# A new order table behind the first transfers in a fused attention and two-MLP kernel

## The chip, the cores and the metric

The kernel runs on one core of a Trainium2 chip. The metric is the device time of one execution in microseconds (us). Five engines work side by side, each through its own queue and in the order of that queue: PE (TensorE, the matmuls), DVE (VectorE), ACT (ScalarE), POOL (GpSimd) and SP (SyncE, which here only issues transfers).

## The reference

Attention over 4 batches, 8 heads, 576 positions and 64 channels, with a causal window; its output is the input of two MLPs, one behind the other, of 2304 rows.

```python
def _attn_ref(q, k, v):
    scores = scale * np.matmul(q, k.transpose(0, 1, 3, 2))
    rel = pos[:, None] - pos[None, :]
    mask_plain = (rel >= 0) & (rel < window)                 # window = 32, heads 0 to 3
    mask_dil = (rel >= 0) & (rel < window * dilation) & (rel % dilation == 0)   # dilation = 4, heads 4 to 7
    ...
    return np.matmul(attn, v)          # softmax of the masked scores, times v

def reference(...):
    x = attn_out.transpose(0, 2, 1, 3).reshape(2304, 512)
    x = np.maximum(x @ moe_w_in, 0.0) ** 2 @ moe_w_out       # 512 -> 2048 -> 512
    h = x @ moe2_w_in                                        # 512 -> 2048
    return (h * (1.0 / (1.0 + np.exp(-h)))) @ moe2_w_out     # -> 512
```

## The kernel before

**Arithmetic.** PE computes with pairs: a fp32 value is held as a hi part (the rounded cast, `copy`, L245 on ACT, L247 on DVE, L249 on POOL) and a lo part (the residual, `sub`, L252, on DVE or POOL). A product is three matmuls: hi·hi, hi·lo, lo·hi. So everything that PE multiplies has to pass through a cast and then a residual on the other engines.

**Weights.** Each piece (one of 16 chunks of 128 hidden columns, input half or output half) arrives as 64-bit numbers and is made into fp32 by integer steps in `weights()`: scale the upper word (L282 on ACT, L284 on DVE or POOL), scale the lower word (L290 on ACT, L292 elsewhere), shift (L302 on DVE or L304 on POOL), set the sign (L311 or L314, DVE), add (L318), then cast and residual. ACT, DVE and POOL can do several of these; the order table picks.

**Attention.** It runs in 8 half-batches of 4 pairs of heads. A block is: scores (L533, PE), mask and row maximum (L558, DVE), exp (L566, ACT), scale (L590 on ACT), transposes, p·v on PE. The first 8 blocks are the "early" ones of `late_exp()`: there the row maximum is subtracted, transposes come first (L713 or L715 and L717) and exp follows them (L729, ACT); p·v is L738 on PE, its row sums are treated at L744 and L746 (DVE), and the normalised result is `xn` (one L751 on DVE, or one L754 for each unit on ACT: three or four). PE transposes `xn` (L625, L630), and a cast and a residual make the MLP's input `x`.

**MLP 1** has tiles of 256, 256, 256, 512, 512 and 512 rows. The first three run chunk by chunk side by side: an up-projection (`s1`, L788 to L790), ReLU (L804) and square (L810) on ACT, cast (L245) and residual (L252) into `g`, a down-projection (`s2`, L836 to L838). Later tiles and MLP 2 (three tiles of 768 rows) use sums of weights that are prepared in between (L389, L417, `st`) so that fewer products are needed (L936, L990 to L992, L1094, L1179). In MLP 2 the Silu (L1130) runs on ACT.

**The order.** Nothing is scheduled at run time. `Planner.order()` (L119) reads the text table `ORDER` (L1358 to L1606): each word is an engine's letter (P, A, V for DVE, G for POOL, D for a transfer), a step's number, and places in memory behind `@`. `run()` (L1308) emits the steps in this order, so an engine's queue is the sequence of its letters. A word `F` is a filler: so many matmuls on a zero tile (L1245), whose result nobody reads. A POOL step waits for the last locked DVE step ahead of it in the table (`turn`). Two dummy activations of one column (L1302 to L1306), one Exp and one Silu, are steps of the table too; the compiler puts an `ACT_TABLE_LOAD` where the needed function changes.

```python
            if word[0] == "F":
                o = self.filler(int(n))
                o.eng = "PE"
            else:
                o = self.ops[int(n)]
                o.eng = {"P": "PE", "A": "ACT", "V": "DVE", "G": "Pool", "D": "DMA"}[word[0]]
```

Of the kernel before, what the change touches and what calls it, by code (L numbers as in the profile page):

```python
# [1359 lines left out]
P10@3 P36@28@1 V17 V50 P67@36@2 G20 A12 V38 A11 V49 V37 D65@156 V48 P13@0 V39 V68 V40 D95@152 P21@1 F3@3 V51 A22  # L1360
P41@2 A23 D96@160 V35 V14 P24@3 V71 A43 V15 G127@0 V70 A42 A16@2 V81 D398@196 V79 P52@1 V69 V82 P44@2 V80 A53
V25 A54 V72 A136@4 P55@0 V26 V45 V66 V46 A27 V83 D143@52 P98@40@3 V56 V138 A47@6 V57 P28@1 G129 P73@3 V100
A29@44 F3@2 V58 A74 V101 D160@76 P59@2 V111 A31@48 V99 P84@3 V32 A62 V30 A60 P75@0 A85 V102 V61 A128 F3@1 V63
V110 D152@56 P86@2 V76 V103 A137 V77 V112 P104@1 A78@8 V113 V87 F7@3 V97 V114 V88 A105 V130 D177@88 A89 P115@1
V139 P106@0 A116 V131 F1@2 P90@3 D169@80 P117@2 V140 A91@60 A93@64 A132@68 F5@1 V94 V92 A141@164 V107 V118
P400@3@1@72@0 V108 V119 D211@124 G133 A153@14 V109@12 V120 A162 V403 F2@2 V401 A145 P121@0 G142 V402 V410
D506@201 P404@2 V411 A122 A144@10 V123 V412 A154 V146 P1238@3 D186@92 V399 A161@2 V147 A170@0 V148 P413@1 A124
A405 V178@4 D220@128 A149@84 V125 V163 A1239@16 P406@0 V150 A414 A1240 V164 P415@2 A179 D194@108 V407 V155
P1244@3 A1241@6 V408 V165 A409@8 V416 V156 A166@100 D424@196 P507@0@1@96@1 V417 V1242 A418 V157 P1243 A1245@18
V167 A158@168 D151 V172 A1246 V510 A187@10 D134 P419@3 V159 P1250@2 A422@104 A420 V512 A1247@12 G189 V508 V423  # L1370
A513 V421 A171 D203@116 V1248 P426@3@0@112@2 V180 A1251@16 V173 A511 P1249 A509 V427 G174 V523 A1252 V428 A188
V429 V436 V438 A1253@14 P430@2 V525 A524 V437 V514 V521 A526 V515 V425 V1254 A522 P439@1 V190 A431 A516 V527
A517 V175@172 P432@3 V528 V176 A440 A529 P518@0 V530 A222 P441@2 V433 V181 A204@2 P531@1 P1255 V434 V442 A520
V182 A435@8 V443 V519 A533 V444 D539@196 A532 A183@120 V191 P534@3 A195@6 V184 P445@0 A537@12 A535 V446 P1256@1
A192@176 G197 V448 V536 A196 V447 D450@201 V449 V198 A205 V193 A1257@18 P540@0@3@20@3 A1258 V199 A1259@4 D237@40
A212@0 V1260 V554 A200@28 P1261 V556 G206 V545 A557 V558 V543 A555 D254@76 V541 V201 A559 P452@0@3@24@0 A542
V560 V207 A544 A546 V561 D538 V451 P1262@1 V208 D271@112 A562 A563 V547 V465 V548 V455 A549 V466 G550 V454
P564@2 V463 A1263@16 D228@36 V464 A565 V456 A1264 V453 A566 V209@180 P551@1 A1265@8 V214 P457@2 A552 A553 V210
A221@14 D245@72 P567@1 V215 A458 A213 V223 P467@0 V1266 A238@12 V216 P459@3 A568 A468 V224 D572@196 A570@4
A217@32 P469@2 V240 A229@10 V225 P1267 A256 V460 V470 V461 V471 G218 V462@6 A239 D478@201 V472 A246@8 V569  # L1380
P473@0 V231 P1274@1 A476@52 A474 V241 A230 V475 A226@184 D262@92 V477 V232 P573@3@0@56@1 A1275@18 V227 A1276
A1277@2 V233 D296@116 A255@6 P480@1@2@80@2 V589 V587 A234@88 G1278 V580 V593 V576 A590 V574 G235 V591 P1279 A247
V483 D305@24 V484 V482 A592 V481 V493 A575 V492 V494 A581 P485@0 V578 V491 A577 D202 V248 A588 V263@10 P495@3
A579 V242 A486 A594 V582 P1286@0 A243@188 V583 D279@108 V479 V595 V584 A272@0 V596 V249 P585@1 V597 A1287@16
P487@2 D219 V244 A586 A496 P598@1 V250 A1288 D571 P497@3 D288@124 A599 V488 A1289@2 V489 P600@0 A490@14 V498
V1290 V499 V251@96 P1291 V257 A500 V252 D605@201 A603@4 V265 P501@2 V258 P1298@1 A504 A502 V601 A280@8 D638@196
V503 V505 V274 P1268@3 V602 A1299@18 V275 A1300 D322@56 A264 V259 P606@2@1@20@3 A273 V266 A1301@12 P1280@0
A1269@16 D604 V611 G281 D313@80 V609 V626 A1270 V620 V624 A610 V607 V267 A625 P1292@3 A1271@2 V613 A260@192 V622
V1302 A290 V261 P1304@2 A1281@18 V282 A612 V1272 A621 V268@128 A1293@16 V276 P639@1@36@0 A1294 A614 V269 A623
P640@3 A627 A1282 V628 V641 P1273 A608 V645 A1283@14 V615 V652 V629 G1284 V616 V654 A630 V643 V656 P1303 V289@2  # L1390
V617 A1305@18 A297@4 V291 V292 P618@0 A1295@6 P1285 A642 V1306 A646 V293 A619 A298 V283 P631@0 P1310@2 A657
V277@132 A653 V284 A632 D339@124 V1296 A285@40 P633@0 V278 A655 V299 P1297 A644 A634 D185 V647 V286 A294@136
A1307@14 V635 D666@201 P1316@1 A1311@16 V306@6 A1312 V648 V658 A636@10 V659 V1308 A660 V295 P1322@2 D287
V1550@12 A649 D637 V308 A1317@18 V1551@2 P661@0 A1313@0 P650@3 P1309 A662 V307 A315 V1314 V1552@112 A651 V324
A1318 P667@3@76@1 V1554@108 A1323@16 V1553 A1324 V300 A1319@8 P663@1 A314@10 V669 P668@0 V1555 V673 A664@2 V1320
P1328@2 V682 V671 V680 D694@196 A672 V684 V316 A674 P1334@3@0@1 V301 A670 A1329@18 V309 A302@72 D665 V675 A1330
P1315 V676 D253 A685 V677 A1559 V303 D330@92 A1331@12 A1556 P678@2 V1332 P1321 V323@0 A1325@14 V317 A681 A679
V1326 A683 P1340@2 V1562@8 A1335@16 A1336 V310 V686 P695@3@20@2 V1563@2 A1341@18 A1342 V687 V1560 A688 P696@2
V701 V703 G1564@116 V697 A702 P1333 V712 A311@144 V714 V1557 A1337@4 D1561 A704 V699 V710 P1327 A715 V325 A700
V1338 V716 V318 D1558 P689@3 A1343@14 V312 P1346@2 A698 A711 V705 V341 A690 V706 V1565 A717 P1352@3 V707  # L1400
A1347@16 A1348 V1566@36 A713 V1344 A319@68 V1567 P708@2 P1339 V326 A709 A1353@18 V320 A1568 D347@112 V718
A1349@2 P691@2 V719 V1574@10 A1354 A1571 V720 P1345 A1355@8 V327 A340@12 A692@6 V342 D726@201 P721@3 V1572
P1358@2 A722 A328@140 V1350 V1575@14 P1364@3 V1356 A1359@16 V329 D1573 A1360 A331@4 V1576@24 V1578@84 P1370@2
A1361@0 V1577 A1365@18 V1569 D693 A1366 A1580 D356@108 V1362 P727@3@80@3 V1579 A1371@16 V343 A1583 P1351 A1372
V733 D1570 V731 V729 V735 V344 A736 P723@2 A734 V1584 A345@148 P728@3 V333 A730 V1581 A1367@10 P1357 A732 V1368
A724@6 V742 D758@196 A332 V746 V737 V748 V744 V357@14 P1382@2 A745 V738 A749 V739 D1585 A743 V334 A747 P740@3
A1383@18 V358 P1363 A741 V335 A1373@2 D364@36 A1384 V750 A336@116 V751 V359 P759@3@2@76@0 V1374 A1385@8 V337
A752 D321 P1369 V773 V762 D725 V760 A348@0 V775 V764 D1582 A761 V1386 P1376@3 V350 A763 V349 A765 V777 A774 V766
V346 D168 A778 P753@2 A1377@16 P1375 V767 V351 A768 A1378 V769 A754 V360 D270 A365@4 P770@2 P1388@3 V1586@10
A1379@6 A776 V771 A772 V361 D236 P755@2 V1380 A1389@18 V779 V1587@12 A1390 P1381 A756@2 V780 V367 D373@56  # L1410
A362@152 V782 A781 V1588@100 V352 P783@2 P1400@3 A784 V1590@20 D390@84 A353@24 V1589 A785 V1591 P1406@2 V354
A1401@16 A1391@10 D757 A1402 V1599@0 D381@92 A1403@12 V1392 P1394@3 A366 V1404 A1407@18 V363 A1595 D789@201 V368
P1387 A1408 A1395@16 V1598@6 A1396 A1409@14 V369 D338 P1418@3 V1410 A370@120 V1600@124 A1592 V1602@80 V1601
P786@2 A1419@18 V371 A1420 P1393 V1603 A1397@8 A787@0 V1398 A1604 V1593 A374@6 D820@196 P1412@3 V1596 A1607
V1605 A1421@10 V391@4 P1399 A1413@16 D1594 V1608 A1414 V393 A1415@2 V383 P790@3@2@108@1 V394 A382@8 D788 A375
D372 V384 P1405 V791 V804 G1416 A792 V806 V795 V793 V808 A794 P1424@3 D355 V376 A796 A807 D1646@112 V797 V798
V1422 P1436@2 V800 A1425@18 V377 A799 A1426 D1609 V1610@12 P801@3 A1437@16 V378 P1411 A802 A803 A809 V1611@0
D1597 A1438 A805 V1614@76 P821@3@2@100@2 A1427@14 V810 V1612@28 V811 P1423 A812 V822 G813 D1606 V824 A823 V826
V828 A825 V1428 A827 V839 P814@3 V835 G1613 V837 P1429 A816 D1655@80 A829 V1615 A815 A1616 V841 V830 V831 A842
P817@3 V832 A1439@0 P833@2 V1440 A818@12 V385 A840 P1442@3 A836 V1623@10 A838 A379@156 V843 V1617 D819 A1619  # L1420
# [253 lines left out]
```

## Time and profile before

| | |
|---|---|
| time, median of 3 runs | 849.27 us (848.89 to 849.51) |
| the profiled execution's own time | 849.5 us |
| its span in the profile | 847.7 us |
| PE busy | 839.2 us (99%) |
| DVE busy | 638.8 us (75%) |
| ACT busy | 501.5 us (59%) |
| POOL busy | 122.2 us (14%) |
| granted TensorE clock, mean | 0.999 |

A busy share is a mean over the whole span. The windows in the rows below give the same for stretches, and the timelines give single instructions: start, duration, engine, line, and in brackets how long the engine had been idle and what ended the idle time. On DVE and ACT neighbours overlap in the record by about 0.1 us, so what a step occupies is read from start to start.

### The profile page before, as it was taken

To read this page: it belongs to the slowest core of one execution; us is meant where nothing else is said; L and a number is where in the kernel's file an instruction comes from. 1 tells how busy PE (TensorE), PEld (TensorE's weight loads), DVE (VectorE), ACT (ScalarE), POOL (GpSimd) and SP (SyncE) were. 2 spreads that over 40 slices of the span, in tenths; PEclk is the share of its full clock that TensorE was granted. 3 is DMA by queue.
4 is the path that set the end of the run, shared out by engine and by line. 5 is a ranking of instruction groups with operands and counts; after the bars stand their busy time and mean duration, and the time that the engine had idled before them with its cause. 6 is when DMAs were issued, how large, how long until landed. Compare 5 with 4: busy or idle time off the path is not lost.

```text
span 847.7 us, 16967 instructions
## 1 busy us (share of the span) xinstructions
PE 839.2 (99%) x6009; PEld 795.6 (94%) x6009; DVE 638.8 (75%) x1706; ACT 501.5 (59%) x1324; POOL 122.2 (14%) x142
## 2 busy tenths in 40 slices
PE   9989999999999999999999999999999999999998
PEld 7879999999989889889998999999999999999998
DVE  6999999888888698768899997578722488422765
ACT  5999988887666265334542566565445555345652
POOL 2220000101210202131201002102201111202020
PEclk9999999999999999999999999999999999999999
DMA  9585568879898888988999989889774774773441
GB/s 344 178 284 207 152 204 304 278 265 333 310 303 318 308 292 282 326 311 288 336 344 299 343 308 351 301 287 324 248 259 149 246 266 164 269 262 111 174 159 65
DMA packets 83603, 223.56 MB, mean 264 GB/s; under 512 B 8768, under 2 KB 18240, under 8 KB 83520
## 3 DMA queue, kind: packets, MB, share of 16 engines
q1 hardware_dynamic: 83520, 222.49, 75.2%
q8 instruction: 47, 0.77, 0.3%
q14 instruction: 36, 0.29, 0.1%
HBM read 172.13 MB, written 50.33 MB: 262 GB/s over the span
## 4 chain that ended last, share of the span: by engine, by line
PE 94%; ACT 3%; DVE 1%; issue 0%; POOL 0%; POOLq 0%; ACTq 0%
PE y L1094 17%; PE sa L1179 15%; PE s L936 15%; PE y L1179 6%; PE y L990 5%; PE y L991 5%; PE y L992 5%; PE sa L1094 4%; PE s L788 3%; PE s L789 2%; PE s L790 2%; PE ax L533 2%; PE y L836 2%; PE ax L625 2%; PE y L837 2%; PE y L838 2%
## 5 line engine op out<-in xcount | busy, mean ns | idle before, releaser
L245 ACT CAST hl<-gq 128x384 fp32r<-128x384 f32 x168 | 79.5, 513 | 58.7 <-PE sa L1179 28.6
L1094 PE MATMUL y<-xs,ws 128*128 128x384 f32 x552 | 107.5, 334 | 0.0
L252 DVE TENSOR_TENSOR hl<-gq,hl 128x384 fp32r<-128x384 f32 x144 | 78.9, 581 | 27.3 <-ACT hl L245 24.0
L1094 PEld LDWEIGHTS y<-xs,ws 128*128 128x128 f32 x552 | 96.6, 188 | 0.1
L1065 DVE TENSOR_TENSOR gq<-y,gq 128x384 f32<-128x384 f32 x46 | 25.0, 554 | 94.1 <-PE y L1094 82.9
L1070 ACT COPY gq<-y 128x384 f32<-128x384 f32 x92 | 42.7, 479 | 75.0 <-PE y L1094 67.6
L1179 PE MATMUL sa<-hl,wp 128*128 128x384 f32 x432 | 79.1, 334 | 0.0
L936 PE MATMUL s<-x,ws 128*128 128x256 f32 x576 | 76.2, 284 | 0.0
L990 PE MATMUL y<-g,w 128*128 128x512 f32 x192 | 76.2, 397 | 0.0
L1179 PEld LDWEIGHTS sa<-hl,wp 128*128 128x128 f32 x432 | 75.2, 188 | 0.0
L991 PE MATMUL y<-g,w 128*128 128x512 f32 x192 | 75.2, 392 | 0.0
L992 PE MATMUL y<-g,w 128*128 128x512 f32 x192 | 74.9, 390 | 0.0
L952 DVE TENSOR_TENSOR h<-s,h 128x512 f32<-128x512 f32 x96 | 59.4, 619 | 19.8 <-PE s L936 16.6
L936 PEld LDWEIGHTS s<-x,ws 128*128 128x128 f32 x576 | 72.2, 191 | 1.2
L245 ACT CAST g<-r 128x256 fp32r<-128x256 f32 (+1 forms) x86 | 42.9, 504 | 51.2 <-DVE r L972 42.8
L566 ACT ACTIVATE ap<-ap,ast 96x128 f32<-96x128 f32 (+3 forms) x168 | 62.2, 371 | 8.3 <-DVE ast L575 4.2
L788 PE MATMUL s<-x,w 128*128 128x256 f32 x192 | 56.4, 294 | 0.1
L790 PE MATMUL s<-x,w 128*128 128x256 f32 x192 | 54.3, 283 | 0.0
L789 PE MATMUL s<-x,w 128*128 128x256 f32 x192 | 54.2, 282 | 0.0
L1179 PE MATMUL y<-hl,sw 128*128 128x384 f32 x288 | 51.4, 334 | 0.0
L1179 PE MATMUL sa<-hl,sw 128*128 128x384 f32 x288 | 50.9, 334 | 0.0
L1179 PEld LDWEIGHTS y<-hl,sw 128*128 128x128 f32 x288 | 50.0, 188 | 0.0
(176 smaller groups left out, 2071.2 us busy)
## 6 DMA issues: line engine op xcount, KB each, us to landing
raw<-w SPq DMA_DIRECT2D x64, 512.0 KB, 6.3
ws<-w1x SPq DMA_DIRECT2D x48, 512.0 KB, 6.7
ws<-w2x SPq DMA_DIRECT2D x48, 512.0 KB, 5.4
sw<-w2y SPq DMA_DIRECT2D x48, 512.0 KB, 4.5
wa<-w1s SPq DMA_DIRECT2D x24, 512.0 KB, 6.8
wa<-w2s SPq DMA_DIRECT2D x24, 512.0 KB, 5.7
w1x<-st SPq DMA_DIRECT2D x16, 512.0 KB, 4.8
w2x<-st SPq DMA_DIRECT2D x16, 512.0 KB, 5.1
```

What stands on the lines that cost most here:

```text
L245: self.nc.scalar.copy(out=out, in_=in_)
L252: self.eng[eng].tensor_tensor(out=out, in0=a, in1=b, op=ALU.subtract)
L566: es.append(self.op({"ACT": c_act(nk) + 0.185}, lambda e, i=i, n=n, c=c, p=p, st=st: nc.scalar.activation(out=p.tile[:n, c], in_=p.tile[:n ...
L788: nc.tensor.matmul(o, wh.tile[:, s], xh, start=(kk == 0), stop=False)
L789: nc.tensor.matmul(o, wh.tile[:, s], xl, start=False, stop=False)
L790: nc.tensor.matmul(o, wl.tile[:, s], xh, start=False, stop=(kk == KC - 1))
L936: nc.tensor.matmul(bank.tile[:, o:o + 256], wp, xp, start=i == 0, stop=last, skip_group_check=True)
L990: nc.tensor.matmul(o, wh.tile[:, s], gh.tile, start=c == 0, stop=False)
L991: nc.tensor.matmul(o, wh.tile[:, s], gl.tile, start=False, stop=False)
L992: nc.tensor.matmul(o, wl.tile[:, s], gh.tile, start=False, stop=(c == NF - 1))
L1094: nc.tensor.matmul(o, w[part == 2].tile[:, kk * P:kk * P + P], x[b][part == 1].tile[:, kk * half:kk * half + half], start=new and not kk a ...
L1179: nc.tensor.matmul(o, u.tile[:, c * P:c * P + P], v.tile, start=new and not q and not part, stop=q == nf - 1 and part == 2, skip_group_che ...
```

## The change

Only the table `ORDER` differs (L1360 to L1606). Its first line and the first words of the next stay, so the first 16 transfers are as before; behind them the words stand in another order. No step is added or removed: 750 PE steps and 516 transfers in both. 182 steps change engine: 81 from ACT to DVE, 55 from DVE to ACT, 36 from POOL to DVE, 10 from POOL to ACT. Steps by engine are 1092 before and 1076 after on ACT, 1479 and 1541 on DVE, 123 and 77 on POOL. The fillers have 53 matmuls before (groups of 14, 15, 3, 3, 3, 7, 1, 5, 2) and 58 after (14, 15, 3, 3, 3, 8, 6, 6), the last six ahead of the down-projection of chunk 3. Places in memory change with the order. The first differing line:

```diff
-P10@3 P36@28@1 V17 V50 P67@36@2 G20 A12 V38 A11 V49 V37 D65@156 V48 P13@0 V39 V68 V40 D95@152 P21@1 F3@3 V51 A22
...
```

Place one, DVE at about 23 to 26 us, ahead of the first up-projection. The row `x<-ax,x 128x4x64` is the last residual of `x` that this up-projection needs; `cv`, `raw` are weight pieces. Before:

```order
L558 ISA ap,ast<-ax,mask 96x128
L558 ISA ast 96x1
L558 ISA ap,ast<-ax,mask 96x128
L558 ISA ast 96x1
L252 TENSOR_TENSOR x<-ax,x 128x4x64
L558 ISA ap,ast<-ax,mask 96x128
L558 ISA ast 96x1
L302 TENSOR_SCALAR cv<-cv 128x512
L510 MEMSET blk 128x6
L311 SCALAR_TENSOR_TENSOR cv<-raw,cv 128x512
L318 ISA cv<-raw,cv 128x1024
L284 TENSOR_SCALAR cv<-raw 128x512
```

In the changed kernel there is first, a little earlier in the queue:

```order
L302 TENSOR_SCALAR cv<-cv 128x512
L252 TENSOR_TENSOR x<-ax,x 128x4x64
L744 TENSOR_SCALAR ast<-ax 72x4
L318 ISA cv<-raw,cv 128x1024
L746 RECIPROCAL ast<-ast 72x4
L510 MEMSET blk 128x6
L744 TENSOR_SCALAR ast<-ax 72x4
L751 TENSOR_TENSOR xn<-ax,ast 72x4x64
L746 RECIPROCAL ast<-ast 72x4
```

and then, around the same residual:

```order
L558 ISA ast 96x1
L558 ISA ap,ast<-ax,mask 96x128
L558 ISA ast 96x1
L311 SCALAR_TENSOR_TENSOR cv<-raw,cv 128x512
L252 TENSOR_TENSOR x<-ax,x 128x4x64
L302 TENSOR_SCALAR cv<-cv 128x512
L558 ISA ap,ast<-ax,mask 96x128
L558 ISA ast 96x1
L318 ISA cv<-raw,cv 128x1024
L311 SCALAR_TENSOR_TENSOR cv<-raw,cv 128x512
```

One `L302` and the `blk` memset stand ahead of the residual now, one `L311` right ahead of it, and the two `xn` are separate, with a row sum's reciprocal between them.

Place two, ACT from about 19 to 25 us. `x<-ax 128x4x64` (the second such row) is the cast whose residual was shown above. Before:

```order
L754 ACTIVATE xn<-ax,ast 72x64 x4
L729 ACTIVATE ap<-ax 72x288
L245 CAST x<-ax 128x4x64
L245 CAST x<-ax 128x4x8
L245 CAST w_467<-cv 128x512
L245 CAST w_478<-cv 128x512
L282 ACTIVATE cv<-raw 128x512
L290 ACTIVATE raw<-raw 128x512 x2
L245 CAST x<-ax 128x4x64
L282 ACTIVATE cv<-raw 128x512
L290 ACTIVATE raw<-raw 128x512
L282 ACTIVATE cv<-raw 128x512 x2
```

After:

```order
L282 ACTIVATE cv<-raw 128x512
L245 CAST x<-ax 128x4x8
L245 CAST x<-ax 128x4x64
L729 ACTIVATE ap<-ax 72x288
L290 ACTIVATE raw<-raw 128x512
L245 CAST w_478<-cv 128x512
L282 ACTIVATE cv<-raw 128x512 x2
L290 ACTIVATE raw<-raw 128x512
L282 ACTIVATE cv<-raw 128x512
L245 CAST x<-ax 128x4x64
L282 ACTIVATE cv<-raw 128x512
L245 CAST w_535<-cv 128x512
```

More `L282` and `L290` weight steps stand ahead of that second cast, and one weight cast (`w`) and one set of four `L754` fewer.

Place three, ACT in the middle of MLP 1, where the dummy Silu (L1304) stands. Before it was much later, ahead of the first `L1130`:

```order
L1070 COPY gq<-y_8110 128x384
L1070 COPY gq<-y_8127 128x384
L245 CAST st<-st 128x2x256 x2
L1304 ACT_TABLE_LOAD
L1304 ACTIVATE first<-warm 128x1
L1070 COPY gq<-sa 128x384
L1130 ACTIVATE gq<-gq 128x768
```

After, with attention's exp (L566) still to come:

```order
L566 ACTIVATE ap,ast<-ap,ast 96x128
L590 ACTIVATE ap<-ap,ast 96x128 x3
L245 COPY ap<-ax 128x288
L1304 ACT_TABLE_LOAD
L1304 ACTIVATE first<-warm 128x1
L245 CAST x_5571<-stg 128x512
L245 CAST x_5581<-stg 128x512
L245 CAST x_5585<-stg 128x512
L245 CAST x_5611<-xr 128x512
```

Some rows later the table for exp is loaded again:

```order
L245 CAST g_5745<-r 128x512
L245 CAST st<-cv 128x512
L245 CAST g_5755<-r 128x512
L245 COPY yo<-y_4323 128x512
L566 ACT_TABLE_LOAD
L566 ACTIVATE ap,ast<-ap,ast 72x104
L245 COPY yo<-y_4284 128x512
L566 ACTIVATE ap,ast<-ap,ast 72x104
```

and once more for Silu, at its first use:

```order
L1070 COPY gq<-y_8205 128x384
L1070 COPY gq<-y_8078 128x384
L1070 COPY gq<-y_8174 128x384
L1130 ACT_TABLE_LOAD
L1130 ACTIVATE gq<-gq 128x768
L245 CAST hl<-gq 128x384
```

So the changed kernel has four table loads, and the one before had two (the other is at the start).

## Rows read from the trace of the kernel before

**Rows 1.** The page: busy tenths in 40 slices, and the chain that ended last.
```profile
PE   9989999999999999999999999999999999999998
PEclk9999999999999999999999999999999999999999
PE 94%; ACT 3%; DVE 1%; issue 0%; POOL 0%; POOLq 0%; ACTq 0%
```

**Rows 2.** Windows: stretch, length, busy (count) of PE, PEld, DVE, ACT, POOL, clock, DMA, GB/s.
```profile
24.80:43.00 18.20, 17.67 (x171) 16.40 (x169) 17.90 (x73) 17.75 (x58) 1.98 (x2) 1.00 0.41 136
43.00:62.00 19.00, 17.34 (x186) 15.03 (x184) 18.72 (x75) 18.71 (x55) 3.56 (x6) 1.00 0.86 287
62.00:75.00 13.00, 12.40 (x133) 11.95 (x135) 12.45 (x58) 11.42 (x43) 1.79 (x2) 1.00 0.89 306
75.00:100.00 25.00, 25.00 (x237) 23.70 (x234) 23.93 (x92) 23.68 (x83) 1.41 (x2) 1.00 0.41 120
100.00:165.00 65.00, 64.88 (x604) 61.90 (x603) 60.30 (x203) 56.11 (x186) 3.20 (x5) 1.00 0.72 252
250.00:400.00 150.00, 150.00 (x1091) 134.00 (x1090) 117.83 (x311) 67.81 (x206) 28.68 (x33) 1.00 0.87 304
400.00:505.00 105.00, 105.00 (x634) 95.28 (x633) 98.38 (x174) 49.12 (x90) 11.91 (x15) 1.00 0.93 328
505.00:848.00 343.00, 339.22 (x1957) 338.81 (x1955) 197.77 (x374) 179.92 (x359) 52.37 (x46) 1.00 0.65 227
```

**Rows 3.** Chain of waits in order of time: start, us, what.
```profile
17.68 0.91 ACT xn L754 x4
...
21.00 0.94 ACT w L245 x2
...
22.51 1.15 ACT raw L290 x2
...
25.43 0.70 DVE cv L311
...
30.75 0.71 ACT xn L754 x3
...
45.93 0.41 ACT g L245
...
61.81 0.73 POOL g L252
```

**Rows 4.** Waits of PE, 0 to 110 us: total us, times, longest.
```profile
PE y L837 <- POOL g L252: 0.9, 1, 0.9
```

**Rows 5.** Timeline of PE: start, duration, what, idle time before it.
```profile
24.32 0.36 PE L788 MATMUL s<-x,w 128*128 128x256 f32 x1
...
46.39 0.38 PE L836 MATMUL y<-g,w 128*128 128x256 f32 x1 [0.82 <-ACT g L245]
...
73.25 0.28 PE L788 MATMUL s<-x,w 128*128 128x256 f32 x1
```

**Rows 6.** Timeline of DVE: start, duration, what, idle time before it.
```profile
22.08 0.75 DVE L751 TENSOR_TENSOR xn<-ax,ast 72x256 f32<-72x256 f32 x2
...
24.22 0.64 DVE L252 TENSOR_TENSOR x<-ax,x 128x256 fp32r<-128x256 f32 x1 [0.30 <-ACT x L245]
24.76 0.28 DVE L558 CUSTOM_DVE_ANT_0 ap<-ax,mask 96x128 f32<-96x128 f32 x1
...
24.97 0.42 DVE L302 TENSOR_SCALAR cv<-cv 128x512 int32<-128x512 int32 x1
...
46.37 0.42 DVE L252 TENSOR_TENSOR g<-r,g 128x256 fp32r<-128x256 f32 x1
...
72.69 0.75 DVE L252 TENSOR_TENSOR x<-ax,x 128x224 fp32r<-128x224 f32 x2
```

**Rows 7.** Groups by line, shapes apart: busy us, mean ns, idle before, releasers.
```profile
L252 DVE TENSOR_TENSOR g<-r,g 128x512 fp32r<-128x512 f32 x39 | 26.9, 694 | 5.2 <-ACT g L245 3.7 <-POOL g L249 1.4
```

**Rows 8.** Timeline of ACT, the load for Silu.
```profile
503.58 1.28 ACT L1304 ACT_TABLE_LOAD   x1
```

## The prediction of the time

> **What bounds the kernel now.** I read the page's slices first. PE is at 9 tenths in nearly every slice and the granted clock is full from the start, so no slice is slow through its clock; PE makes 94% of the chain that ended last [rows 1]. The total can therefore change only where PE waits, or where something new makes it wait. The windows say where that is [rows 2]. From 24.8 to 43 us PE is busy 17.67 of 18.20, from 43 to 62 us 17.34 of 19.00, from 62 to 75 us 12.40 of 13.00; from 75 to 100, 250 to 400 and 400 to 505 us every microsecond. So PE loses 0.53 + 1.66 + 0.60 = 2.8 us between 24.8 and 75 us, and after 75 us it goes from one matmul to the next. Whatever lateness PE has at 75 us it still has at the end, and the work order behind that point can only add to it.
>
> In the opening the feeders are full: DVE is busy 17.90 of 18.20 and 18.72 of 19.00 us, ACT 17.75 and 18.71 [rows 2]. The chain there goes through ACT and DVE by turns, on ACT at 30.75 and still at 45.93 us, on POOL at 61.81 [rows 3], and after 64 us it stays on PE. PE's longest wait of these, 0.9 us, is for a residual from POOL [rows 4], the next, 0.82, for a hi cast of ACT and the residual behind it. As marks I use three PE rows: the first up-projection of MLP 1 at 24.32 us, the down-projection of chunk 3 at 46.39 after 0.82 idle, and the up-projection that needs the last early attention pair at 73.25 [rows 5].
>
> **The change, part by part.** Nothing is computed more or less: 750 PE steps and 516 transfers stay, 182 steps change engine (81 ACT to DVE, 55 DVE to ACT, 36 POOL to DVE, 10 POOL to ACT), and order changes on every engine from about 17 us. PE gets 53 warm-up fills before and 58 now. Net, DVE gets 62 more steps.
>
> (1) To the first up-projection. It waits for an ACT cast of x and then for the DVE residual of x at 24.22, which had 0.30 idle ahead of it for that cast [rows 6]. Ahead of the cast ACT now does one more `L290` and three more `L282`, steps that stand behind it before; it drops one weight cast and one set of four small `L754`. In the chain two `L290` take 1.15, two such casts 0.94, four `L754` 0.91 [rows 3], so with `L282` priced as `L290`, its twin: 4 x 0.575 = 2.30 in, 0.47 + 0.91 = 1.38 out, +0.9. Ahead of the DVE residual the new order puts an `L302` (0.42 in the record, 0.35 without the overlap with its neighbour), an `L311` (0.70), a memset (under 0.1), one `L751` that ACT did as four `L754` (two take 0.75, so 0.35) and 0.1 less of the `L558` [rows 3, 6]: +1.4, or +1.1 if the idle takes 0.30. So the first up-projection comes +0.9 to +1.4 later; I take +1.2, at 25.5 us.
>
> (2) To chunk 3's down-projection. Its last feeder is DVE's `L252` residual at 46.37, behind ACT's cast at 45.93 [rows 3, 6]. Ahead of that residual come three `L751` (0.35 each), a cast and a scaling of the same size (0.35 each) and four `L558` (0.21 each, from 24.76 to 24.97 [rows 6]): 2.6. Five casts and scalings leave for ACT, three at 0.35 and two narrow ones at 0.1 to 0.15: 1.3. That is +1.3. The idle of DVE is 0.30 of 18.20 and 0.28 of 19.00 us [rows 2], so +0.7 to +1.3 stays by this count. Following the steps of the new order one after the other, each with its row's duration, I get +1.5, since two of the residual's feeders are now late as well; I take +1.4.
>
> (3) To the last early pair. The `L252` rows at 72.69 end the wait for 73.25 [rows 5, 6]. Ahead of them come twelve steps new to that stretch: four `L751` (1.4), three weight scalings that ACT did (1.05), one `L311` (0.6 without overlap) and four copies, casts and scalings, 1.7 in all, taken between the 0.35 of the `L302` row and the 0.64 of the `L252` row at 24.22 [rows 6]: 4.7. Out go one `L311` (0.6) and eight casts and scalings, mostly at 0.35 and two of them narrow (2.4): 3.0. Net +1.7. DVE idles 0.30 + 0.28 + 0.55 = 1.1 us in the three windows [rows 2]. If all of it were closed, +0.6 stays; if none, +1.7. ACT's queue up to there gets 2.2 shorter (six fewer casts and `L754` sets than come in). Following the steps I reach this up-projection 1.4 late. **Term: +1.4, bounds +0.6 and +1.7.** The fills cost nothing by themselves: the new six stand ahead of chunk 3's down-projection, where PE is idle 0.82 us [rows 5]; should its feeder come early, they are on the path. A fill is 256 columns wide like the matmul at 73.25, recorded with 0.28 [rows 5]; matmuls overlap, so six cost less than 1.7.
>
> (4) From 75 to 165 us. DVE is at 23.93 of 25.00 and then 60.30 of 65.00 us, PE at 25.00 and 64.88 [rows 2]. So DVE idles 1.1 and 4.7 us there and PE 0.1. The residuals that chunks need stand 2 to 5 us of work deeper in the new DVE queue, and this idle, together with the lead that DVE has on PE, takes most of it; counted with all idle closed, the worst place, near 117 us, is still 0.7 late. Bounds 0 and +2 (half of what is moved in front at the deepest place, rounded down), taken as +0.6, near the closed count.
>
> (5) 300 to 505 us. From 400 us on DVE is busy 98.38 of 105.00 us, POOL 11.91 [rows 2]. Twenty steps come to DVE and four leave: thirteen ACT steps (mostly weight scalings, 0.35 on DVE where ACT needs 0.575) and seven of POOL (`L252` on 512 columns takes 694 ns on DVE, 0.6 without the overlap [rows 7]). Sixteen net, between 0.35 and 0.6, are 5.6 to 9.6, and with the mix as it is 6.5: 104.9 of 105. The cover is the stretch ahead: DVE is busy 117.83 of 150.00 there [rows 2] and the weight steps may run early. Taken as 0; bounds 0 and +4.
>
> (6) Table loads. The dummy Silu is moved from 503.58 to about 320 us. There are Exp activations behind it, so a load for Exp follows, and another for Silu ahead of the first `L1130`: four loads for two. A load takes 1.28 [rows 8]. ACT is busy 67.81 of 150.00 us in that stretch [rows 2], so the two extra are hidden; cost 0, bounds 0 and 2.6. The Trainium skill (page "ScalarE: Activation LUTs", section "What ACT_TABLE_LOAD costs") speaks against this part: it counts about 2.66 us for a switch of sets, load and drain together. By that page the upper bound would be 5.3 rather than 2.6. The row here shows 1.28 and no drain; whether one lies on ACT when work is queued on both sides, no row of this trace shows.
>
> (7) After 505 us DVE is busy 197.77 of 343.00 and takes over 19 POOL steps, about 11 us; this is free. What PE idles there (3.8 us) lies at the last tile, whose order of feeders stays.
>
> **Sum.** The profiled run took 849.5 us, 0.2 above the median of 849.27. 849.5 + 1.4 + 0.6 = 851.5, and 0.2 less for a median: **851.3 us**, with bounds 849.9 (0.6 + 0) to 853.0 (1.7 + 2).
>
> **Rivals.** *Not slower: ACT was the true bound.* The chain passes through ACT from 30.75 us on, and ACT's queue gets shorter: 0.6 by 50 us, 2.2 by 73 us. If DVE can close its idle by being fed sooner, its lateness vanishes where ACT's goes, and PE picks up some of the 2.8 us that it waits. Price: -0.6 to -2.2, middle -1, so 848.3 us. For it: the ACT rows in the chain. Against: DVE has only 1.1 us of idle to close against 1.7 us of new work. It decides if the up-projection of 73.25 comes at or before 73.2. *DVE becomes the bound at 400 to 505 us:* part (5) is not covered and PE shows waits for `L252` or `L318`: +2 to +4, so 853.3 to 855.3 us. It decides where DVE reaches 400 us without a lead of 8. *The table loads lie on the path:* +2.6, 853.9 us; it decides if PE shows a wait right behind the load for Exp. *The clock drops in the opening:* the granted clock was 1.00 in all windows [rows 2], and where PE runs at the lower level it takes the time twice; one or two us of that would give 852.5 to 853.5. *The change doesn't do what it says:* direct pairs of dependent steps get more, not fewer (111 to 138 on DVE, 33 to 52 on ACT), and the clock was already full, so neither aim has much to win; this stands within the forecast.
>
> **How the numbers follow.** Forecast 0.44; not slower 0.38; DVE bound 0.10; table loads 0.05; clock 0.03. About 0.2% (1.7 us, so 847.6 to 851.0) is what a measurement of this kernel can tell from no change. Of the forecast's own 849.9 to 853.0, a third lies below 851.0: 0.14 same, 0.30 slower. Of the first rival 0.28 is same and 0.10 faster, since its better end passes 847.6. The other three, 0.18, are slower. Faster 0.10, same 0.42, slower 0.48. The range for 8 in 10 reaches from 847.8, just above where the first rival counts as faster, to 854.5, into the second rival; the forecast's own range is 849.9 to 853.0.
>
> **What would show it.** Right: first up-projection near 25.5, chunk 3's down-projection near 47.8, the up-projection of the last pair near 74.7 us, with DVE at 99% between 25 and 75 us, and PE busy in every later stretch but for 0.6 us before 165. Wrong: these marks at or ahead of 24.3, 46.4 and 73.2 (first rival); PE below 104.5 of 105 from 400 to 505 us (second); PE idle behind the load for Exp (third); a clock under 1.00 in the opening (fourth).

## The result and the profile after

The changed kernel takes 860.29 us (median of 4 runs, 858.96 to 862.98) against 849.08 (848.75 to 849.51): ratio 1.0136, with a 95% interval of 1.0109 to 1.0162. It is slower, by 11.2 us where 2.0 were forecast, and lies above the forecast's range of 849.9 to 853.0 and the wider one of 847.8 to 854.5. The profiled execution took 862.98 us. Of the experiments below, e1 and e9 each had one disturbed run (1049 and 3963 us), which is left out; it was the profiled one, so neither has a profile to read.

The page of the changed kernel: span and busy times, the granted clock in slices, and the chain's first line.

```profile
span 861.2 us, 16904 instructions
PE 845.5 (98%) x6014; PEld 800.5 (93%) x6014; DVE 665.0 (77%) x1768; ACT 494.4 (57%) x1304; POOL 90.1 (10%) x93
PEclk9889999999999999999999999999999999999999
PE 86%; DVE 3%; DMA 2%; ACT 1%; issue 1%; POOL 0%; SPq 0%; POOLq 0%; ACTq 0%; DVEq 0%
```

Two things are new against [rows 1]: the second and third slice of the clock are below 9, and transfers are in the chain. The windows, with the columns of [rows 2]:

```profile
20.00:24.80 4.80, 3.83 (x35) 2.62 (x34) 4.36 (x23) 4.16 (x8) 1.28 (x1) 0.76 0.88 284
24.80:43.00 18.20, 17.65 (x149) 16.78 (x148) 17.13 (x62) 15.32 (x44) 6.43 (x4) 0.88 0.70 250
43.00:62.00 19.00, 16.16 (x160) 14.45 (x159) 16.00 (x65) 15.27 (x51) 3.75 (x3) 0.95 0.71 254
62.00:75.00 13.00, 12.57 (x118) 12.09 (x117) 10.88 (x59) 10.23 (x33) 3.27 (x3) 0.81 0.55 170
75.00:100.00 25.00, 24.53 (x245) 23.24 (x243) 24.12 (x85) 22.97 (x79) 1.41 (x2) 1.00 0.28 88
165.00:250.00 85.00, 83.48 (x787) 78.60 (x786) 72.11 (x250) 61.89 (x210) 7.63 (x9) 1.00 0.77 271
250.00:400.00 150.00, 147.43 (x1096) 131.12 (x1096) 121.37 (x330) 70.38 (x220) 16.03 (x19) 1.00 0.83 292
400.00:505.00 105.00, 105.00 (x637) 94.21 (x636) 99.50 (x178) 39.08 (x72) 7.80 (x7) 1.00 0.93 333
505.00:848.00 343.00, 343.00 (x1975) 341.95 (x1974) 221.40 (x425) 186.35 (x374) 35.10 (x28) 1.00 0.68 239
```

PE loses 2.84 us from 43 to 62 us (1.66 before), 1.52 from 165 to 250 and 2.57 from 250 to 400, where before it lost nothing from 250 to 400; and it runs at a clock below 1.00 in four windows up to 75 us. From 400 us on it waits for nothing again, until the last tile. DVE and ACT are not full in the opening: 16.00 and 15.27 of 19.00 us, where [rows 2] have 18.72 and 18.71.

A selection of what PE waits for, in total us, times, longest; [rows 4] had one longest wait of 0.9:

```profile
PE ax L602 <- POOL ap L592: 1.8, 1, 1.8
PE s L936 <- issue: 1.7, 1, 1.7
PE ax L533 <- DMA blk<-qkv: 1.0, 1, 1.0
PE s L936 <- DMA ws<-w1x: 0.6, 1, 0.6
```

The trace of before has none of these four: a POOL scaling, a block of attention's input, weights of MLP 1, and, behind the word "issue", a raw weight piece that is told below. The three marks of [rows 5] in the changed kernel: first up-projection, chunk 3's down-projection, the up-projection that needs the last early pair.

```profile
26.56 0.56 PE L788 MATMUL s<-x,w 128*128 128x256 f32 x1
...
50.27 0.38 PE L836 MATMUL y<-g,w 128*128 128x256 f32 x1
...
80.44 0.28 PE L788 MATMUL s<-x,w 128*128 128x256 f32 x1
```

They are 2.2, 3.9 and 7.2 us late. The first matmul is recorded with 0.56 where [rows 5] have 0.36: PE is at the lower level there. So 7.2 of the profiled run's 13.5 us of extra span (861.2 against 847.7) stand at 80 us.

**The POOL scaling.** `L592` scales the scores of one block, two instructions. In the trace of before, POOL and what DVE did beside it:

```profile
50.62 0.72 POOL L592 TENSOR_SCALAR ap<-ap,ast 96x128 f32<-96x128 f32 x2 [3.07 <-ACT ap L590]
...
51.06 0.26 DVE L558 CUSTOM_DVE_ANT_0 ap<-ax,mask 72x104 f32<-72x104 f32 x1
```

In the changed kernel, POOL, DVE beside it, and PE:

```profile
54.73 2.69 POOL L592 TENSOR_SCALAR ap<-ap,ast 96x128 f32<-96x128 f32 x2 [4.38 <-ACT ap L590]
...
55.30 0.42 DVE L284 TENSOR_SCALAR cv<-raw 128x512 f32<-128x512 f32 x1
55.64 0.68 DVE L311 SCALAR_TENSOR_TENSOR cv<-raw,cv 128x512 int32<-128x512 int32 x1
56.26 0.68 DVE L252 TENSOR_TENSOR w<-cv,w 128x512 fp32r<-128x512 f32 x1
...
57.48 0.30 PE L602 MATMUL ax<-ident,ap 96*128 96x96 f32 x1 [1.80 <-POOL ap L592]
```

The same two instructions take 2.69 us where they took 0.72. Their single records (least, median and greatest duration in ns), before and changed:

```profile
L592 POOL TENSOR_SCALAR ap<-ap,ast x2: 369/370/370, 50.6 to 51.0; 96x128 f32<-96x128 f32 x2
L592 POOL TENSOR_SCALAR ap<-ap,ast x2: 372/1356/2341, 54.7 to 55.1; 96x128 f32<-96x128 f32 x2
```

In the changed kernel the first of the two takes 0.37 us, while DVE is still at `L558`, and only the second, from 55.1 us on, takes 2.34. Before, DVE went on with `L558`, which reads scores from PSUM; now it goes on with weight steps that read and write SBUF, and POOL ends only after them. The Trainium skill (page "GPSIMD Engine Reference", section "1. Specifications") says that POOL shares its SBUF interface with VectorE and contends with DVE instructions of two SBUF inputs or of a two-port mode. The two pairs of rows agree with it.

**The clock behind it.** Windows of 5 us behind that wait:

```profile
55.00:60.00 5.00, 3.20 (x40) 2.76 (x39) 3.29 (x12) 3.20 (x11) 2.42 (x2) 1.00 0.81 311
60.00:65.00 5.00, 5.00 (x34) 5.00 (x33) 3.89 (x13) 3.65 (x9) 1.28 (x1) 0.50 0.02 10
```

PE is busy 3.20 of 5 us, and in the next 5 us the granted clock is 0.50, the lower of its two levels, with 34 matmuls where PE is busy all the time. The four runs of the changed kernel have mean clocks of 0.992, 0.996, 0.998 and 0.998 at 862.98, 861.10, 859.47 and 858.96 us; the runs of before beside the experiments have 0.998 to 1.000. A clock of 0.992 in place of 0.998 is 0.006 x 861 = 5 us of work at full speed, and the runs differ by 4.

**The transfers.** For PE's wait of 1.0 us at 237.4, the chain in order of time (start, us, what):

```profile
229.32 0.70 DVE h L952
230.02 0.08 SPq L348
...
230.16 0.43 SPq L853
...
231.16 7.19 DMA blk<-qkv
...
238.48 0.94 PE ax L533 x16
```

The block is issued at 231.16, behind others in SP's queue, and lands at 238.34. `SPq` is SP's queue, which stands still until its next transfer may start: its place has been read out, or its data is there. From 225 to 232 us it waited 2.3 us for a matmul (`L936`) and 1.2 for a DVE residual. For the longest, 1.7 us at 386.4, PE waits for a DVE step, and DVE for a raw weight piece:

```profile
386.55 0.43 DVE L284 TENSOR_SCALAR cv<-raw 128x512 f32<-128x512 f32 x1 [2.22 <-DMA raw<-w]
386.89 1.14 DVE L952 TENSOR_TENSOR h<-s,h 128x256 f32<-128x256 f32 x2
```

```profile
388.13 0.95 PE L936 MATMUL s<-x,wa 128*128 128x256 f32 x6 [1.71 <-issue]
```

The profile names "issue", since the releaser is not plain; the last of the `L952` steps that free a bank ends at 388.03, 0.1 before PE goes on, and `L284` stands ahead of it in DVE's queue.

### The profile page after: what moved, and what is told of

Read it like the earlier page. It is cut to its first block, busy times and chain, and to the rows that moved or that the text cites. A ratio compares the mean times of both kernels' runs of the same rounds, so it can differ in the third digit from the quotient of the medians.

```text
span 861.2 us, 16904 instructions
## 1 busy us (share of the span) xinstructions
PE 845.5 (98%) x6014; PEld 800.5 (93%) x6014; DVE 665.0 (77%) x1768; ACT 494.4 (57%) x1304; POOL 90.1 (10%) x93
## 4 chain that ended last, share of the span: by engine, by line
PE 86%; DVE 3%; DMA 2%; ACT 1%; issue 1%; POOL 0%; SPq 0%; POOLq 0%; ACTq 0%; DVEq 0%
PE y L1094 17%; PE sa L1179 15%; PE s L936 13%; PE y L1179 6%; PE y L990 5%; PE y L991 5%; PE y L992 5%; PE sa L1094 4%; PE s L788 2%; PE s L790 2%; PE s L789 2%; PE ax L533 2%; PE y L836 2%; PE y L837 2%; PE ax L625 2%; PE y L838 1%
## 5 line engine op out<-in xcount | busy, mean ns | idle before, releaser
L245 ACT CAST hl<-gq 128x384 fp32r<-128x384 f32 x168 | 77.4, 512 | 43.7 <-DVE gq L252 28.3
L252 DVE TENSOR_TENSOR hl<-gq,hl 128x384 fp32r<-128x384 f32 x158 | 82.3, 557 | 21.5 <-ACT hl L245 21.3
L936 PE MATMUL s<-x,ws 128*128 128x256 f32 x576 | 75.3, 284 | 0.6 <-DMA ws<-w1x 0.6
L245 ACT CAST g<-r 128x256 fp32r<-128x256 f32 (+1 forms) x90 | 45.0, 509 | 52.6 <-DVE r L972 45.8
L936 PEld LDWEIGHTS s<-x,ws 128*128 128x128 f32 x576 | 71.9, 192 | 1.7 <-DMA ws<-w1x 0.8
L566 ACT ACTIVATE ap<-ap,ast 96x128 f32<-96x128 f32 (+3 forms) x168 | 62.3, 372 | 15.4 <-DVE ast L558 15.3
L952 DVE TENSOR_TENSOR h<-s,h 128x512 f32<-128x512 f32 x96 | 59.6, 621 | 10.7 <-PE s L936 5.0
L788 PE MATMUL s<-x,w 128*128 128x256 f32 x192 | 57.3, 299 | 0.6 <-DVE xo L247 0.3
L789 PE MATMUL s<-x,w 128*128 128x256 f32 x192 | 55.0, 286 | 0.0
L790 PE MATMUL s<-x,w 128*128 128x256 f32 x192 | 54.9, 286 | 0.0
L252 DVE TENSOR_TENSOR g<-r,g 128x256 fp32r<-128x256 f32 (+1 forms) x88 | 48.8, 559 | 3.8 <-ACT g L245 2.7
```

The costliest lines, as they stand in the source:

```text
L245: self.nc.scalar.copy(out=out, in_=in_)
L252: self.eng[eng].tensor_tensor(out=out, in0=a, in1=b, op=ALU.subtract)
L566: es.append(self.op({"ACT": c_act(nk) + 0.185}, lambda e, i=i, n=n, c=c, p=p, st=st: nc.scalar.activation(out=p.tile[:n, c], in_=p.tile[:n ...
L788: nc.tensor.matmul(o, wh.tile[:, s], xh, start=(kk == 0), stop=False)
L789: nc.tensor.matmul(o, wh.tile[:, s], xl, start=False, stop=False)
L790: nc.tensor.matmul(o, wl.tile[:, s], xh, start=False, stop=(kk == KC - 1))
```

## The experiments

Each is told against 860.29 us of the changed kernel and 849 of before (848.90 to 849.35 in the three sets). The changed kernel's own ratio is 1.0109 to 1.0162, so an edit is clear of it only when its interval lies outside that.

**e1, fills in PE's gaps.**

```diff
-A116 P117@2
+A116 F8@1 P117@2
...
-A566 P551@3
+A566 F14@3 P551@3
```

> The changed kernel with two more groups of fills, 8 ahead of the fourth p·v of the early blocks (PE waited 0.91 us there, at 20.3 us) and 14 ahead of the transposes that waited 1.8 us for POOL (at 55.9 us). Theory (PE's waits in the opening let the clock fall, and that is what varies from run to run): the granted clock stays at 1.00 in every window of the opening, the clock mean is 0.998 or more in all runs, and the time is 858 to 859 us, 1 to 2 under the changed kernel's 860.3. Rival (the waits themselves cost, the clock little): 860 to 861.5, since 22 fills add up to 2.6 us where PE does not wait.

The three runs are 858.43, 859.27 and 859.75 us; ratio 1.0121 (1.0104 to 1.0138). The mean clock is 0.999 in all three, as the theory said, where the changed kernel's runs have 0.992 to 0.998. The middle time lies between the theory's range and the rival's, and the interval overlaps that of the changed kernel, so the fills held the clock up but their gain, 1.0 us by the medians, is not clear of the noise.

**e2 and e3, order and engines apart.** In e2 the letters of 182 words of the old table are those of the changed one, with the old places; in e3 the reverse.

> The order of before, with the engines of the changed kernel for all 182 moved steps. Theory (the order costs, not the engines): 849 to 852 us, PE busy without a gap from 100 to 505 us. Rival (DVE's 62 more steps are the cost, as in my forecast's terms): 854 to 860 us, with DVE at 99% from 25 to 75 us and PE waiting for DVE there.

> The order of the changed kernel, with the engines of before. Theory (the order costs): 857 to 862 us, with PE waits for transfers between 230 and 390 us as in the changed kernel. Rival (the engines cost): 849 to 853 us.

e2 took 861.43 us (ratio 1.0142, 1.0125 to 1.0160), e3 900.26 (1.0615, 1.0590 to 1.0640). Both theories fall, and both rivals too: either half alone is as slow as both or much slower. In e2 PE waits mostly for ACT, not for DVE, and it waits where neither kernel does, 75 to 165 us; the windows of e2:

```profile
75.00:100.00 25.00, 23.90 (x225) 23.01 (x224) 22.83 (x79) 20.92 (x73) 1.40 (x2) 1.00 0.48 149
100.00:165.00 65.00, 61.85 (x557) 58.07 (x557) 57.57 (x191) 54.03 (x172) 1.49 (x2) 1.00 0.65 223
```

As I read it, an engine choice fits one order. So the question "order or engines" has no answer here, and the loss has to be followed wait by wait.

**e4, the Silu load back.**

```diff
-V1771 A1161 A3959 A2114@116
+V1771 A1161 A2114@116
...
+P2819 A2820 A3959 A2818
```

> The changed kernel with the dummy Silu put back right ahead of the first Silu, so two table loads in all. Theory (the two extra loads are hidden): 859.5 to 861 us. Rival (a load lies on the path): 857 to 858 us, 2.6 less.

861.07 us (ratio 1.0146, 1.0130 to 1.0161): at the upper end of the theory's range, and far from the rival's. The two extra loads cost nothing that can be measured. In the changed kernel the load for Exp is followed at once by the exp, 0.02 us behind its end:

```profile
339.17 1.28 ACT L566 ACT_TABLE_LOAD   x1
340.47 0.38 ACT L566 ACTIVATE ap<-ap,ast 72x104 f32<-72x104 f32 x1
```

e4 shows one thing more. Its table is the changed one up to about 320 us, but in its profiled run the clock was 1.00 in the windows from 20 to 43 us, where the changed kernel's had 0.76 and 0.88. Its marks:

```profile
24.73 0.36 PE L788 MATMUL s<-x,w 128*128 128x256 f32 x1
...
48.10 0.38 PE L836 MATMUL y<-g,w 128*128 128x256 f32 x1
...
79.09 0.28 PE L788 MATMUL s<-x,w 128*128 128x256 f32 x1
```

The changed kernel's marks are 1.8, 2.2 and 1.4 us behind these. That is what the lower clock between 20 and 43 us cost that one run.

**e5, two POOL steps to DVE.** `G142` and `G550` become `V142` and `V550`.

> The changed kernel with two POOL steps of its opening given to DVE: the weight residual L252 that took 2.85 us on POOL at 26.8 us (1.28 before the change), and the pair of L592 scalings that took 2.69 us at 54.7 us (0.72 before) and for which PE waited 1.8 us. Theory (POOL is slowed by what DVE does beside it, and that is one of the opening's losses): the 1.8 us wait goes, and with it the stretch at a clock of 0.50 behind it; 856.5 to 859 us. Rival (DVE is the bound, and 1.2 us more on it eat the gain): 860 to 861.5 us.

862.45 us (ratio 1.0156, 1.0138 to 1.0174), above both ranges: no gain, as the rival said, but for another reason. From 43 to 62 us PE is busy 17.94 of 19.00 in place of 16.16, so the scaling's gain is there; from 24.8 to 43 us it is busy 15.57 in place of 17.65. There DVE stands still:

```profile
26.03 0.69 DVE L252 TENSOR_TENSOR w<-cv,w 128x512 fp32r<-128x512 f32 x1 [1.90 <-ACT w L245]
...
27.45 0.59 DVE L252 TENSOR_TENSOR x<-ax,x 128x256 fp32r<-128x256 f32 x1
```

The weight residual, put in DVE's queue where POOL had it, waits for a cast that ACT does only at 25.39 us, and the residual of `x`, for which PE waits 1.7 us, stands behind it. The edit mixed a good step with a bad one, so the two were taken apart in e9.

**e6, other places for 53 transfers.** The first and the last words:

```diff
-D1646@112
+D1646@110
...
-D2537@40
+D2537@100
```

> The changed kernel with 53 transfers between 160 and 420 us put at other places in memory, ones whose earlier contents were read out sooner; order and engines untouched. Theory (transfers land late because each waits for its place, and that makes PE wait between 230 and 390 us): transfers land earlier, PE's 4 us of waits from 165 to 400 us shrink to 1 or less, and the time falls to 856.5 to 858.5 us. Rival (transfers are late through the order of the queue or through late data, not through places): 859.5 to 861 us, with the waits where they were.

890.37 us (ratio 1.0488, 1.0465 to 1.0511): both missed. PE waits 9.1 us for `ws`, 3.8 for a block and 1.9 for `wc`. Each new place was free earlier for its own transfer, but, as I read it and did not test, whatever used that place next then waited longer. The edit is no repair, and it does not show that places cause the waits of the changed kernel. What it shows is that places alone, with the order and the engines as they are, move the time by 30 us. Theory and rival stay undecided by it.

**e7 and e8, the tables spliced at the up-projection of chunk 7.**

> The changed table up to the up-projection of chunk 7 (78.9 us), then the steps that are left in the order and with the engines of before (99 of 1528 places had to be chosen anew). Theory (loss in two parts, opening with its clock, and late transfers behind it): the opening's part alone, 852.5 to 856 us, PE without a wait from 165 to 505 us. Rival (the loss lies behind the opening): 849.5 to 851.5 us.

> The table of before up to the same up-projection (71.7 us there), then the steps that are left in the order and with the engines of the changed kernel (485 places chosen anew). Theory: the second part alone, 852 to 856 us, with PE waits between 75 and 400 us and a full clock up to 75 us. Rival (all is lost in the opening, and what follows only carries it on): 849 to 850.5 us.

e7 took 861.96 us (ratio 1.0158, 1.0143 to 1.0173), above both ranges. PE is busy 19.73 of 25 us from 75 to 100 us, because one block transfer that the old order issues earlier stands behind the seam (a wait of 5.3 us); from 250 to 505 us PE has no gap, and from 165 to 250 us one of 0.12 in all, as the theory said. Without that wait it would be at 856.7, an estimate (861.96 - 5.3), 7.8 over its set's before (848.90), with a mean clock of 0.992 in the profiled run: about the opening's 7.2 of the marks. e8 took 960.93 us and is full of waits for transfers (13.2 us for blocks, 21.3 for `ws`, 21.5 for `sw`), as I read it from the places chosen anew. It says nothing on the changed kernel's rest.

**e9, the scaling alone to DVE.** `G550` becomes `V550`.

> The changed kernel with the one pair of L592 scalings given to DVE (one L586), the weight residual left on POOL. Theory (POOL's 2.69 us for 0.72 held PE, and the wait brought the clock down behind it): PE is busy 17.5 us or more from 43 to 62 us instead of 16.16, the clock is 1.00 in the windows from 43 to 75 us, and the time is 857.5 to 859.5 us. Rival (DVE is full and gives the wait back elsewhere): 860 to 861.5 us, with PE busy under 17 us there.

858.69 us (856.87 to 859.76 in four runs; ratio 1.0100, 1.0081 to 1.0120), in the theory's range. Their mean clocks are 0.995 to 1.000. The interval overlaps that of the changed kernel, so the gain of 1.6 us is not clear of the noise by itself. What the theory said of the windows is seen in e11 and e12, which hold the same edit: PE is busy 17.96 and 17.95 us from 43 to 62, and the clock is 1.00 from 43 to 75.

**e10, three transfers ahead.**

```diff
-D2127@51 D1691 A941 D1531 D1537 D967@196
+D967@196 D2127@51 D1691 A941 D1531 D1537
...
-D2337@60 P2373 P2377 V1186 V2389 V1200 D1207@196 D2303 D2336@98
+D2336@98 D2337@60 P2373 P2377 V1186 V2389 V1200 D1207@196 D2303
...
-D1823@37 D2304@84 D1206 D2347@13 D2350@76 D1814@72
+D1814@72 D1823@37 D2304@84 D1206 D2347@13 D2350@76
```

> The changed kernel with three transfers moved ahead in the queue, past one that waits for its place: the block for which PE waited 1.0 us at 237.4, the weights for which it waited 0.6 at 349, and the raw piece for which DVE, and behind it PE, waited at 386 (1.7 us). Engines, places and all other steps as they were. Theory (late transfers, held up behind another at the head of SP's queue, cost the 4 us between 165 and 400): PE is busy 149.5 us or more of 150 from 250 to 400 us instead of 147.43, and the time is 856.5 to 858.5 us. Rival (the next transfer is late then): 859.5 to 861 us.

858.65 us (ratio 1.0107, 1.0091 to 1.0123), 0.15 above the theory's range, and an interval that overlaps that of the changed kernel; the waits of the profile show the gain better. The three waits are gone; one of 1.1 us for a DVE scaling (`L586`) has come in their place, so PE is busy 148.89 us from 250 to 400 and not the expected 149.5. Its windows:

```profile
165.00:250.00 85.00, 84.50 (x796) 79.64 (x795) 73.00 (x256) 63.12 (x216) 9.16 (x9) 1.00 0.78 275
250.00:400.00 150.00, 148.89 (x1109) 132.78 (x1108) 122.12 (x329) 70.08 (x215) 16.01 (x19) 1.00 0.83 294
```

PE's loss in the two windows falls from 1.52 + 2.57 to 0.50 + 1.11 us, by 2.5. Its opening is as the changed kernel's (clock 0.76, 0.88, 0.95 and 0.81 in the same windows).

**e11, both.**

> Both edits: the scaling on DVE and the three transfers ahead. Theory (two separate losses, each on PE's path): the gains add up, 854.5 to 857.5 us. Rival (one hides the other): as the better of the two alone.

855.72 us (ratio 1.0079, 1.0062 to 1.0097), in the theory's range and clear of the changed kernel's interval. Neither edit hides the other: 1.6 us each by the medians, 4.6 of the 11.2 together. The clock is at 1.00 in every window of the opening, and the mean clock 0.999 in the profiled run. Its windows and its marks (PE):

```profile
24.80:43.00 18.20, 17.18 (x159) 16.00 (x158) 17.58 (x70) 16.76 (x51) 10.30 (x4) 1.00 0.78 285
43.00:62.00 19.00, 17.96 (x190) 15.77 (x188) 17.45 (x70) 16.67 (x51) 2.33 (x2) 1.00 0.71 246
62.00:75.00 13.00, 11.67 (x133) 10.92 (x130) 12.83 (x60) 11.49 (x39) 2.03 (x2) 1.00 0.56 194
```

```profile
24.88 0.36 PE L788 MATMUL s<-x,w 128*128 128x256 f32 x1
...
48.25 0.39 PE L836 MATMUL y<-g,w 128*128 128x256 f32 x1
...
75.37 0.28 PE L788 MATMUL s<-x,w 128*128 128x256 f32 x1
```

At a full clock and without the scaling the marks of [rows 5] are 0.6, 1.9 and 2.1 us late.

**e12, both and eight fills** (`F8@1` ahead of `P117@2`).

> Both edits and 8 more fills ahead of the fourth p·v of the early blocks, where PE waited 0.91 us. Theory (what is left of the clock's loss follows the waits near 20 us): no window from 20 to 43 us has a clock under 0.95, the mean clock is 0.998 or more in every run, and the time is 0.5 to 2 us below that of both edits alone. Rival (the fills do nothing but delay): 0 to 1 us above it.

856.29 us (ratio 1.0081, 1.0066 to 1.0097), 0.6 above e11, and the same within the intervals: the rival. The theory's clock came true (0.998 to 1.000 in all five runs, where one of e11's five had 0.995 and took 858.28 us), but the time did not fall: in e11's profiled run the clock was already full, so there was nothing left for fills to hold up. No kernel here beats the one before.

## Why the prediction was wrong

The sum had +1.4 us at the third mark, +0.6 from 75 to 165 us, and nothing behind that. In the profiled run the third mark is 7.2 us late; PE then loses 0.5 us up to 165 us, and 4.1 us from 165 to 400 us, for which the sum has no term. Two steps failed: POOL's durations were taken as fixed, and the queue of transfers was put at nothing without a reason. A third failed with them: a wait of PE was priced at its own length, without the clock.

**What bounds the kernel: right in part.** PE's waits decide, and what stands behind 75 us could only add. It added. But the total does not change only where PE waits: at the lower clock PE's own work took longer.

**Terms 1 to 3, the opening's order: near in size once the rest is taken off, but not for the stated reason.** The forecast had the marks 1.2, 1.4 and 1.4 us late; e11, where POOL's scaling and the clock are out of the way, has them 0.6, 1.9 and 2.1 late. The first is under its bounds of 0.9 and 1.4, the third above its upper bound of 1.7. That the sizes are near is partly luck, since the marks were read wrongly. The prediction has the first and the third wait for a DVE residual. [rows 5] have no idle time ahead of either, and by [rows 6] the residuals end behind the marks: 24.22 + 0.64 = 24.86 against 24.32, and 72.69 + 0.75 = 73.44 against 73.25. At the second mark the idle time ends with ACT's cast, as its row says, when the residual (46.37) has only begun. The changed kernel's new waits ahead of the first mark stand earlier and are for ACT; the longest:

```profile
21.18 0.73 PE L738 MATMUL ax<-w,ap 72*72 72x65 f32 x8 [0.91 <-ACT ap L729]
```

The picture beside it was wrong too: DVE was to be at 99%, and in the changed kernel it is busy 16.00 of 19.00 us from 43 to 62, in e11 17.45.

**The step that failed first: durations of POOL were taken as fixed.** The prediction walked DVE's and ACT's queues and gave POOL's steps of the opening no term. But where the scaling now stands, DVE works on SBUF beside it, and 0.72 became 2.69. PE waited 1.8 us, and more came behind: the third mark is at 79.09 in e4, with the scaling on POOL, and at 75.37 in e11, with it on DVE, while the first two marks of these runs agree within 0.2. So 3.7 us at the third mark are the wait and what it brought, in one profile of each; by the end less of it is left, as e9's median is 1.6 us under the changed kernel's and e11's 2.9 under e10's. With the 2.1 of e11 and the 1.4 that the clock cost the profiled run earlier, this makes up the 7.2. The trace of before had a sign of it: of its twelve POOL records of `L592` the median is 0.35 us and the longest 1.23, with DVE's `L302` and `L972` beside it.

**The clock's rival was named with 0.03, and a wait was priced at its own length.** (Its price, 852.5 to 853.5, also adds one or two us to 851.5 and not to the forecast's 851.3.) In the profiled run, PE's busy time rose by 6.4 us (839.2 to 845.5) with five more fills, and most of that is matmuls at the lower level, around 25 us and behind the wait at 57. In the runs with a mean clock of 0.998 this part is smaller, so by run it is between 1 and 6 us, an estimate (0.001 to 0.007 of 860, against the 0.999 of before). The two stretches are of different kinds. Behind POOL's wait the clock fell in every profile that has it: the changed kernel, e4, e6, e7 and e10 are below 1.00 both from 43 to 62 and from 62 to 75 us (0.81 to 0.95), and e5, e11 and e12, without it, are at 1.00 in both. The fall near 20 us comes and goes from run to run: the windows from 20 to 43 us are at 0.76 and 0.88 in the changed kernel and e10 and at 1.00 in e4 and e6, with one table and the same waits up to there.

**The step that was missing: the transfers.** The section on the change says that the first 16 are the same; the prediction counts 516 in both and prices nothing behind them. It took SP's queue as a bystander. That queue is in order, each transfer waits at its head until its place is free, and the new table has other places and another order of transfers. e10 moves three words past others and changes nothing else, and PE's loss between 165 and 400 us falls by 2.5 us. That the places are what made those transfers late in the first place was argued, and e6 did not show it.

**Term 4, 75 to 165 us: right in size.** PE loses 0.5 us there (0.6 forecast), but from 75 to 100 us (24.53 of 25.00) and not near 117. **Term 5 and the second rival, DVE from 400 to 505 us:** DVE is at 99.50 of 105.00 and PE at 105.00; the work did move ahead, as the cover said. **Term 6, table loads:** hidden (e4). **Term 7:** free; PE is busy 343.00 of 343.00 from 505 to 848 us, and what it idles stands behind that, at the last tile, as before.

**The first rival, not slower because ACT is relieved:** no. ACT is busy 15.27 of 19.00 us where it was 18.71, and PE gains nothing.

**What stays open.** e11 is 6.4 us above before. Some 2.1 stand at 75 us; PE's gaps from 75 to 400 us are 0.49 + 0.71 + 0.67 + 1.11 = 3.0 in its windows, against 0.1 before from 75 to 165, and 0 from 165 on. The rest, 1.3 to 1.4, has no one place; PE's busy time alone is 841.0 us in e11 and 839.2 before, and what in it is longer was not followed. The 4.6 us of e11's edits are shown by runs; the 2.1 at the third mark are counted but not taken apart.

## What to carry to other kernels

When a change rewrites the order of a kernel in which four engines and a queue of transfers are tuned to each other, cost the queue of transfers as well as the engines: list for each stage how long ahead of its use a transfer lands, and what stands at the queue's head. A duration is read beside the neighbours of its trace, so look at what stands beside a POOL step in the new order, and at the longest record of its line in the old trace. A row that starts beside a mark does not hold it: look for idle time ahead of the mark. And a wait of PE can cost more than its length, so look at the granted clock in the windows that follow, and in more than one profile.

## What the runs showed of the hardware

POOL's stretch was larger than expected. A weight residual (`L252`, 128x512) that takes 1.28 to 1.30 us on POOL in the opening of before took 6.50 in e11, beside DVE's weight steps. Two rows of e11, the first with attention steps beside it:

```profile
22.37 1.28 POOL L252 TENSOR_TENSOR w<-cv,w 128x512 fp32r<-128x512 f32 x1 [7.69 <-DVE blk L510]
26.05 6.50 POOL L252 TENSOR_TENSOR w<-cv,w 128x512 fp32r<-128x512 f32 x1 [2.40 <-DVE cv L302]
```

The second is 2.85 in the changed kernel's profile and 6.52 in e4's, with the same table up to there: what stands beside it in that run decides, as I read it. A later pair of `L592` on POOL takes 0.37 for each in the changed kernel (168.0 us), and in e11 (162.9 us) 0.37 and 1.86, for which PE waits 0.9.

It seems to go the other way too: in the changed kernel a DVE step on three columns, 0.16 to 0.17 elsewhere, is recorded with 1.26 while POOL does `L318` and `L304`. One record shows it, and no run tested it:

```profile
36.96 1.26 DVE L573 TENSOR_SCALAR ast<-ast 96x3 f32<-96x3 f32 x1
```

And the clock's lower level came behind a short loss: PE was idle 1.8 us in the stretch from 55 to 60 us, and the next 5 us ran at 0.50. It did not come behind every loss: from 20 to 24.8 us PE is busy 3.83 us in the changed kernel and 3.78 in e4, and the clock is 0.76 and 1.00.
